# A linear-attention and feed-forward kernel on one core: raw weight loads opened by ScalarE, the first output cut in two, GpSimd's fills reordered, and another order of the first four steps

## The chip, the core and the metric

The kernel runs on one core of one Trainium2 chip. Five engines work side by side, each through its own queue of instructions in order: TensorE (PE, matrix products), VectorE (DVE, elementwise), ScalarE (ACT, activations and copies), GpSimd (POOL, fills, copies and some loads) and SyncE (SP, which issues most transfers). An instruction starts when it is first in its engine's queue and the semaphores that it waits for have been raised. Transfers between the chip's memory (HBM) and the core's (SBUF) run on 16 DMA engines, whichever engine issues them. Products land in PSUM.

The metric is the device time of one execution, in microseconds (us).

## The reference

The first half is a gated linear recurrence for 4 sequences with 8 heads, 768 positions and 48 channels; the second is a feed-forward layer on 3072 rows of 384, with a hidden width of 2048.

```python
f = 1.0 / (1.0 + np.exp(-f_logit))
state = np.zeros((B, H, D, D), dtype=np.float32)
for t in range(S):
    state = f[:, :, t, :, None] * state + np.einsum('bhd,bhe->bhde', k[:, :, t], v[:, :, t])
    y[:, :, t] = np.einsum('bhd,bhde->bhe', q[:, :, t], state)

x = y.transpose(0, 2, 1, 3).reshape(B * S, H * D)
h = x @ w_in
g = np.maximum(h, 0.0) + alpha * np.minimum(h, 0.0)
out = g @ w_out
```

Everything is float32. The rows of x that a position gives depend on all earlier positions of its sequence through `state` alone, so the positions are cut into chunks.

## The kernel before

**Steps.** The 768 positions are cut into 6 chunks of 128, the 4 sequences into 2 pairs. A step is one chunk of one pair; there are 12, numbered 0 to 11, the two pairs alternating. Steps 0 and 1 are the first chunks, which have no earlier state. Each step has these parts, generators that yield between pieces:

- P (`prepare`): loads of f, q, k and v (in steps 1 to 4 from GpSimd's queue, in the others from SP's), the sigmoid, and the products of gates over runs of 4 and 32 positions. It fills the tiles `kr`, `qd`, `us`, `ps`, `ss`, `k4`, and from them `q3`, `ks`, `kh`.
- S and T (`scores`, one for each sequence of the pair): products of keys and queries inside blocks of 32 positions (line 580), laid by masked copies on VectorE (L589 with the mask `mraw`, L615 with `mhalf` in first chunks, L599 with `mquad` in later ones) into `ad`.
- O (`carry`): products across blocks (L490, L512), the chunk's keys transposed (L529), the new state's part (L543), and `moved(0)`, which brings the state `vs` forward, in first chunks by ScalarE copies (L559).
- Y (`attend`): copies of `ad` into the attention matrix `A` (L623), the output of the attention (L634), its copy (L641), `moved(1)` on VectorE (L553, L557), and x transposed: in step 0 by products with a shifted identity `dense` (L653), in all others by small transfers (L664).
- K and M (`keys_moved`, `landed`): in later chunks the keys go through SBUF-to-SBUF transfers (L464).
- n (`network`): the feed-forward layer. Eight pieces of 12 matmul records (L679), each with ScalarE's `neg` (L684) and VectorE's `gate` (L686), and then products with `w_out`: in step 0 plain (L699), in the others by a scheme with 7 half-size products in place of 8 (L718).

**Weights.** w_in and w_out each come in 8 raw loads on SP's queue (L234) into 3 staging buffers. Of each, ScalarE makes a rounded float32 and a half-precision correction (L238, L239), and VectorE adds them as integers (L248). In the order the letters are a (raw load and ScalarE's two) and w (VectorE's) for w_in, b and g for w_out, W for sums of w_out's quarters (L784). A one-element ScalarE copy into the first staging buffer (L303, with q as its source) makes the first raw load wait until q has come.

**Order.** TensorE, VectorE, ScalarE and SP run a hand-made order: the string `START` is read word by word and each word advances one generator (`P0:4` advances P of step 0 four times). Steps from the fifth on follow a repeated pattern, `USUAL`. GpSimd is not in that list; its instructions stand in an order that a scheduler makes from the program's order. Fillers on TensorE, i (one product of 256 columns) and j (16 very small ones), write to a bank that nobody reads.

```python
        for key in ORDER:
            next(run[key] if key in run else pieces[key[0]])
```

**GpSimd before the first loads.** Its program is a row of fills and copies that build masks and zeros: `kr`, `fs`, `ones`, `mraw`, `mquad` (L171, L175), `mhalf` (L178, L183), `ad`, `A` (L190), the identity, `dense` (L197, L199); the fills of `us` for step 0 (L335, L336: zeros and ones in two parts of the tile) come from P, and so do the loads of the second step (L284, L293).

Of the kernel before, what the change touches and what calls it, by code (L numbers as in the profile page):

```python
# [8 lines left out]
F32 = mybir.dt.float32  # L9
I16 = mybir.dt.int16  # L10
# [7 lines left out]
C = 128  # L18
DB = 32
MASKED = (1, 0)  # L20

U = 2
CH = 64
NC2 = C // CH
NB = DB // 4
WP = 768
RAWS, LEADS = 3, 4
# [1 line left out]

BEGUN = 5  # L30
START = (
# [7 lines left out]
)  # L39
USUAL = "T:2 S:2 n:4 M T:2 S n P+ S n P+ n:3 Y O P+ O:2 Y O n P+ Y:2 P+ n:3 P+:3 K+"  # L40

LOOSE = ("a", "w", "b", "g", "W", "i", "j", "X")

def flat(start, usual, steps=12):
    out = []
# [15 lines left out]
def kernel(  # L61
# [30 lines left out]
    nc = tc.nc  # L92
    B, NC, _, HP, _ = qT.shape
    DM = v.shape[-1]
    H = 2 * HP
# [66 lines left out]

    mraw = const.tile([128, 4, NB, 4], F32, tag="mraw", name="mraw")
    nc.gpsimd.memset(mraw, 0.0)
    diag = lvl[:, 1].rearrange("p (i r) -> p i r", r=4)
    for d in range(4):
        nc.gpsimd.tensor_copy(mraw[:, d, :, d:4], diag[:, :, 0:4 - d])
    inq = const.tile([128, NB], F32, tag="inq", name="inq")
    nc.vector.tensor_reduce(inq, diag, mybir.AxisListType.X, ALU.add)
    mquad = const.tile([128, UW], F32, tag="mquad", name="mquad")  # L170
    nc.gpsimd.memset(mquad, 0.0)  # L171
    for m in range(1, NB):
        lo = UO[m] + (4 if m == 1 else 0)
        n = NB - m
        nc.gpsimd.tensor_copy(mquad[:, lo:lo + 4 * n].rearrange("p (i r) -> p i r", r=4),  # L175
                              inq[:, 0:n].unsqueeze(2).broadcast_to((128, n, 4)))
# [24 lines left out]
    first = {"raw": stage.tile([128, WP, 4], I16, tag="raw", name="w_in_raw0", bufs=RAWS)}  # L201

    def load_weights(dst, src, name):

        rows_ = NK if dst is w_in_sb else 1
        pieces_ = dst.shape[1] * dst.shape[2] // WP
        if rows_ == 1:
            dst = dst.rearrange("p a n -> p (a n)").unsqueeze(1)
        width = WP // rows_
        words = src.rearrange("p (a n) -> p a n", a=rows_).bitcast(I16)  # L220
        got = {}

        def of(n):
            return dst[:, :, n * width:(n + 1) * width]

        def by_row(t):
            return t.rearrange("p (a n) -> p a n", a=rows_)

        def upper(n):
            if not n and dst is w_in_sb:  # L230
                raw = first["raw"]
            else:
                raw = stage.tile([128, WP, 4], I16, tag="raw", name=f"{name}_raw{n}", bufs=RAWS)
            nc.sync.dma_start(out=raw.rearrange("p (a n) four -> p a (n four)", a=rows_)[:, :, 0:4 * width - 1],  # L234
                              in_=words[:, :, 4 * n * width + 1:4 * (n + 1) * width])

            lead = stage.tile([128, WP], F16, tag="lead", name=f"{name}_lead{n}", bufs=LEADS)
            nc.scalar.activation(lead, raw[:, :, 2].bitcast(BF16), AF.Copy, scale=0.5)  # L238
            nc.scalar.activation(as_int(n, I32), by_row(raw.bitcast(U32)[:, :, 0]), AF.Copy, scale=2.0 ** -13)  # L239
            got[n] = lead  # L240

        def as_int(n, dtype):
            t = of(n).bitcast(dtype)
            return t if dtype is I32 else t.rearrange("p a (n two) -> p a n two", two=2)[:, :, :, 1]

        def both(n):
            t = by_row(got.pop(n).bitcast(I16))
            nc.vector.tensor_tensor(as_int(n, I16), as_int(n, I16), t, ALU.add)  # L248
# [23 lines left out]
    def prepare(bp, c, x):  # L272
# [27 lines left out]
        qdv = [qd[:, :, QO[d]:QO[d] + NB * (4 - d)].rearrange("p g (i r) -> p g i r", r=4 - d) for d in range(4)]  # L300
        nc.scalar.copy(qd[:, :, 0:DB], q.rearrange("p (g t) -> p g t", t=DB))
        if not ahead:
            nc.scalar.copy(first["raw"].rearrange("p n four -> p (n four)")[:, 0:2].bitcast(F32), q[:, 0:1])  # L303
# [21 lines left out]


        ps = work.tile([128, NS], F32, tag="ps", name=f"ps_{i}", bufs=1)
        ut = work.tile([128, G * UW], F32, tag="us", name=f"us_{i}", bufs=1)
        if c:
            us = ut.rearrange("p (g t) -> p g t", g=G)  # L330
        else:

            at = (0, VW, VW + 16, VW + 16 + DB, VW + 16 + DB + NB)
            us, q16, k16, g16 = (ut[:, G * lo:G * hi].rearrange("p (g t) -> p g t", g=G) for lo, hi in zip(at, at[1:]))
            nc.gpsimd.memset(k16[:, :, 16:DB], 0.0)  # L335
            nc.gpsimd.memset(g16[:, :, 3:5], 1.0)  # L336
# [139 lines left out]
    def carry(bp, c, x):  # L476
# [21 lines left out]
        f64 = work.tile([128, U, H], F32, tag="f64", name=f"f64_{i}")  # L498
# [119 lines left out]
    def attend(bp, c, x):  # L618
# [5 lines left out]
            if j % 2:  # L624
                yield

        py = (more if (bp, c) == steps[0] else pairs)[0]
        for u in range(U):
            for hp in range(HP):
                for cc in range(NC2):  # L630
                    for par in range(2):
                        hd = 2 * hp + par
                        o = hp * C + CH * cc
                        nc.tensor.matmul(py[64 * par:64 * par + 64, u, o:o + CH],  # L634
                                         lhsT=vs[bp][:, cc, u, hd * D:hd * D + 64],
                                         rhs=A[:, u, par * HP + hp, CH * cc:CH * (cc + 1)],
                                         start=True, stop=True)
# [237 lines left out]
```

## Time and profile before

| | us |
|---|---|
| median of 3 runs | 602.92 (602.43 to 603.97) |
| the profiled execution | 602.81 |
| its span, first to last instruction | 601.0 |
| TensorE busy in the span | 575.6 (96%) |
| VectorE busy | 494.7 (82%) |
| ScalarE busy | 247.4 (41%) |
| GpSimd busy | 85.4 (14%) |

In the page's table of slices every digit is the busy share, in tenths, of one of 40 equal slices of the span, some 15 us each. The chain is the work that ended last, followed back from the last instruction. A row of the timeline gives the start in us from the beginning of the span, the duration, the engine, the line, the operation, the tile written and those read, the shapes, how many were merged, and in brackets the engine's idle time before the row and who ended it. A float32 matmul leaves two records, a transpose one. From about 120 us on the steps follow each other every 46.4 us (the products of L679 begin at 235.5, 281.9 and 328.4 us in steps 4, 5 and 6).

### The profile page before, as it was taken

The page shows a single profiled execution, that of the slowest core. Times are in us where ns is not written, and L with a number is a line of the kernel's source. Part 1 is how long each engine was busy: PE and PEld are TensorE (multiplying, and loading weights), DVE is VectorE, ACT ScalarE, POOL GpSimd, SP SyncE. Part 2 cuts the span into 40 slices and gives each one's busy share as a digit, 9 for nine tenths or more (in the row PEclk, how much of TensorE's full clock was granted, in tenths as well). Part 3 has the DMA queues.
Part 4 walks back from the last instruction along what each step waited for, and adds up shares of the span by engine and source line. Part 5 has one row for each costly group of instructions (what it writes and reads, how often), then busy time and mean ns, then how long its engine had stood idle before and what let it go on. Part 6 is the DMA issues. An engine that isn't in the chain of part 4 may idle for free.

```text
span 601.0 us, 18092 instructions
## 1 busy us (share of the span) xinstructions
PE 575.6 (96%) x7760; PEld 516.8 (86%) x7760; DVE 494.7 (82%) x998; ACT 247.4 (41%) x430; POOL 85.4 (14%) x162
## 2 busy tenths in 40 slices
PE   2489999999999999999999999999999999999997
PEld 1378667898899899899899899899899899899997
DVE  7989998997888779988988988988988987882351
ACT  5679952621461450550461451452343344232110
POOL 9210014013002103001200300300300300300000
PEclk9999999999999999999999999999999999999999
DMA  8778736015005302502601601601601511201000
GB/s 263 254 216 295 249 89 125 1 48 130 2 2 161 52 1 59 156 1 56 157 2 55 159 3 56 158 2 41 170 4 30 155 31 27 55 1 29 27 1 27
DMA packets 52880, 50.36 MB, mean 84 GB/s; under 512 B 26720, under 2 KB 43360, under 8 KB 52800
## 3 DMA queue, kind: packets, MB, share of 16 engines
q1 hardware_dynamic: 42784, 37.46, 21.7%
q0 software_dynamic: 5504, 9.90, 6.7%
q10 hardware_dynamic: 4512, 1.85, 1.3%
q8 instruction: 61, 1.00, 0.7%
q14 instruction: 19, 0.16, 0.1%
HBM read 36.21 MB, written 4.72 MB: 68 GB/s over the span
## 4 chain that ended last, share of the span: by engine, by line
PE 88%; DVE 7%; ACT 2%; POOL 1%; issue 1%; DMA 0%; DVEq 0%; ACTq 0%; POOLq 0%
PE ph L679 40%; PE pa L718 10%; PE pc L718 10%; PE pair L580 6%; PE pe L718 5%; PE pd L718 5%; PE pb L718 5%; PE pair L634 3%; PE pair L543 1%; DVE w_out_sb L248 1%; PE pair L512 1%; PE po L699 1%; DVE gate L686 1%; POOL mhalf L183 1%; DMA f<-in_fT 0%
## 5 line engine op out<-in xcount | busy, mean ns | idle before, releaser
L679 PE MATMUL ph<-xT,w_in_sb 128*128 128x256 f32 x1152 | 255.3, 381 | 1.4 <-DVE w_in_sb L248 1.4
L679 PEld LDWEIGHTS ph<-xT,w_in_sb 128*128 128x128 f32 x1152 | 216.9, 190 | 33.4 <-issue 2.4
L686 DVE SCALAR_TENSOR_TENSOR gate<-neg,om,ph 128x256 f32<-128x256 f32 x192 | 81.2, 476 | 33.0 <-ACT neg L684 33.0
L684 ACT ACTIVATE neg<-ph 128x512 f32<-128x512 f32 x96 | 56.1, 594 | 121.2 <-PE ph L679 101.6
L718 PE MATMUL pa<-w_out_sb,gate 128*128 128x192 f32 x352 | 62.1, 330 | 0.0
L718 PE MATMUL pc<-t,S 128*128 128x192 f32 x352 | 61.6, 328 | 0.0
L454 ACT COPY A<-q 48x512 f32<-48x512 f32 x44 | 27.1, 617 | 83.4 <-DVE q L408 82.9
L718 PEld LDWEIGHTS pa<-w_out_sb,gate 128*128 128x128 f32 x352 | 57.4, 190 | 1.3
L464 POOL DMA_DIRECT2D ksn<-kt x80 | 46.2, 586 | 85.9 <-DVE kt L422 61.3
L718 PEld LDWEIGHTS pc<-t,S 128*128 128x128 f32 x352 | 57.4, 190 | 0.4
L664 POOL DMA_DIRECT2D xT<-y x22 | 11.9, 544 | 287.5 <-ACT y L641 287.4
L599 DVE COPY_PREDICATED ad<-mquad,pair 128x224 f32<-128x224 int32 (+6 forms) x140 | 41.7, 299 | 4.1
L589 DVE COPY_PREDICATED ad<-mraw,pair 128x256 f32<-128x256 int32 (+1 forms) x96 | 41.2, 451 | 4.0 <-PE pair L580 0.8
L364 DVE TENSOR_TENSOR us<-us,fs 128x768 f32<-128x768 f32 (+5 forms) x60 | 36.9, 615 | 1.1
L765 DVE TENSOR_TENSOR S<-gate 128x512 f32<-128x512 f32 x44 | 30.3, 688 | 0.8
L718 PE MATMUL pe<-w_out_sb,S 128*128 128x192 f32 x176 | 30.6, 327 | 0.0
L718 PE MATMUL pb<-t,gate 128*128 128x192 f32 x176 | 30.4, 326 | 0.0
L718 PE MATMUL pd<-w_out_sb,S 128*128 128x192 f32 x176 | 30.4, 326 | 0.0
L623 ACT COPY A<-ad 32x512 f32<-32x512 f32 x48 | 29.4, 613 | 0.6
L641 ACT COPY y<-pair 128x512 f32<-128x512 f32 x22 | 11.8, 589 | 43.4 <-PE pair L634 43.4
L718 PEld LDWEIGHTS pe<-w_out_sb,S 128*128 128x128 f32 x176 | 28.8, 190 | 0.2
L718 PEld LDWEIGHTS pb<-t,gate 128*128 128x128 f32 x176 | 28.9, 190 | 0.0
(125 smaller groups left out, 710.6 us busy)
## 6 DMA issues: line engine op xcount, KB each, us to landing
w_out_raw<-in_w_out SPq DMA_DIRECT2D x8, 767.8 KB, 7.9
w_in_raw<-in_w_in SPq DMA_DIRECT2D x8, 767.2 KB, 9.5
out<-o SPq DMA_DIRECT2D x23, 192.0 KB, 1.9
q<-in_qT SPq DMA_DIRECT2D x8, 512.0 KB, 4.6
k<-in_kT SPq DMA_DIRECT2D x8, 512.0 KB, 7.1
f<-in_fT SPq DMA_DIRECT2D x7, 512.0 KB, 3.9
vs<-in_v SPq DMA_DIRECT2D x16, 192.0 KB
ksn<-kt SPq DMA_DIRECT2D x80, 32.0 KB, 2.2
```

Of the source, the lines that this page charges most:

```text
L364: nc.vector.tensor_tensor(us[:, :, UO[m]:UO[m] + 4 * n].rearrange("p g (i r) -> p g i r", r=4), us[:, :, skip:skip + 4 * n].rearrange("p g ...
L454: nc.scalar.copy(A[halves(cc)[1], :, par * HP:(par + 1) * HP, CH * cc:CH * (cc + 1)], q3[rows(par)].rearrange("p (u h c) s t -> p u h c (s ...
L464: (nc.gpsimd if a % 2 else nc.sync).dma_start(out=ksn[32 * b:32 * (b + 1)].rearrange("p u (h x) -> p (u h) x", h=HP)[:, :, 32 * a:32 * a + n],
L580: nc.tensor.matmul(to[DB * j:DB * (j + 1), par, hp * step + lo:hp * step + hi], lhsT=keys[r_, g * DB:(g + 1) * DB], rhs=by[r_, g, lo:hi], ...
L589: nc.vector.copy_predicated(adu[:, :, :, d:4], mraw[:, d, :, d:4].bitcast(I32).unsqueeze(1).broadcast_to((128, H, NB, n)), rv[:, :, QO[d]: ...
L599: nc.vector.copy_predicated(ad[:, u, :, :, 4 * m:DB], mquad[:, lo:lo + n].bitcast(I32).unsqueeze(1).unsqueeze(1).broadcast_to((128, 2, HP, ...
L623: nc.scalar.copy(A[s_].rearrange("p u h t -> p (u h) t")[:, :, s_], ad[s_].rearrange("p u r h t -> p (u r h) t"))
L679: nc.tensor.matmul(ph[:, j * T:(j + 1) * T], lhsT=w_in_sb[:, kt, m * 128:(m + 1) * 128], rhs=xT[:, kt], start=(kt == 0 and j == 0), stop=( ...
L684: nc.scalar.activation(neg, phv, AF.Relu, scale=-1.0)
L686: nc.vector.scalar_tensor_tensor(gate[:, m % NH, m // NH], neg[:, j], om[:, m:m + 1], phv[:, j], ALU.mult, ALU.add)
L718: nc.tensor.matmul(to[:, 0:DH], lhsT=of(f), rhs=by(f), start=(f == 0 and not more), stop=(f == NH - 1), skip_group_check=True)
L765: nc.vector.tensor_tensor(to, x_, y_, op)
```

## The change

It has four parts and an order.

- The first three raw tiles are made beforehand, and a function `opened` writes one element of a tile from ScalarE. The first is opened with q as before; a new letter e opens the second and third, with `inq` as the source, at two places of the order.
- The tile `us` of step 0 is made before the masks, and its two fills (`of_halves`) stand ahead of them; the fill of `A` goes to the end of the masks, and `mquad` is made in `quads_of_mask`, called in P of step 1 behind its loads.
- In step 0 the output of the attention (L634) is made in two halves of 16 matmuls, first the first half of the chunk for all heads, with a yield between.
- `START` is another order of steps 0 to 4. The filler j is gone from it, and both fillers i stand at its head.

```diff
-    "i P0:4 j T0 P0:2 S0 P0 a O0:2 T0 P1 P0 O0 T0 S0 O0 P1 S0 a O0 P1 T0 S0 P1 O0:2 Y0 i P1 Y0 O0 S1 w Y0 "
-    "a Y0 X a w O1 Y0 w O1 w S1 P1 a n0 w a:2 P1 n0 a T1 P1 P2 b S1 T1 S1 n0 w:2 n0 T1 O1 P2 T1 b P2 n0 w "
+    "P0 i P0 i P0 S0 P0:2 O0 e P0 O0 a P0 T0 e w P1 O0 T0 O0 a P1 O0:2 S0 T0:2 S0:2 P0 O0 P1 Y0 P1 Y0:2 "
+    "O0 Y0 a P1 Y0 P1 O1 a w X Y0 O1 w n0 a T1 S1:2 w:2 n0 a P2 w T1 P2 P1 a S1 n0 a S1 w n0:2 b T1 b O1 "
...
+    def of_halves(ut):
+
+        parts = [ut[:, G * lo:G * hi].rearrange("p (g t) -> p g t", g=G) for lo, hi in zip(at, at[1:])]
+        nc.gpsimd.memset(parts[2][:, :, 16:DB], 0.0)
+        nc.gpsimd.memset(parts[3][:, :, 3:5], 1.0)
+        return parts
+
+    first = {"us": work.tile([128, G * UW], F32, tag="us", name="us_first", bufs=1)}
+    first["parts"] = of_halves(first["us"])
...
-    nc.gpsimd.memset(mquad, 0.0)
-    for m in range(1, NB):
...
-    nc.gpsimd.memset(A, 0.0)
...
+    nc.gpsimd.memset(A, 0.0)
+
+    first["raw"] = [stage.tile([128, WP, 4], I16, tag="raw", name=f"w_in_raw{n}", bufs=RAWS) for n in range(RAWS)]
+
+    def opened(n, by):
+
+        nc.scalar.copy(first["raw"][n].rearrange("p n four -> p (n four)")[:, 0:2].bitcast(F32), by)
+
+    def quads_of_mask():
+
+        nc.gpsimd.memset(mquad, 0.0)
+        for m in range(1, NB):
+            lo = UO[m] + (4 if m == 1 else 0)
+            n = NB - m
+            nc.gpsimd.tensor_copy(mquad[:, lo:lo + 4 * n].rearrange("p (i r) -> p i r", r=4),
+                                  inq[:, 0:n].unsqueeze(2).broadcast_to((128, n, 4)))
...
+        if ahead == 1:
+            quads_of_mask()
...
+        chunks_first = (bp, c) == steps[0]
+        py = (more if chunks_first else pairs)[0]
+        each = [(u, hp, cc) for u in range(U) for hp in range(HP) for cc in range(NC2)]
+        for n, (u, hp, cc) in enumerate(sorted(each, key=lambda x: x[2]) if chunks_first else each):
+            if chunks_first and n == U * HP:
+                yield
...
+    pieces["e"] = (opened(n, inq[:, 0:1]) for n in range(1, RAWS))
```

More of the change, by code (lines that the diff above doesn't have):

```diff
@@ L31 @@
 START = (
[7 rows of a table removed]
[7 rows of a table added]
 )
 USUAL = "T:2 S:2 n:4 M T:2 S n P+ S n P+ n:3 Y O P+ O:2 Y O n P+ Y:2 P+ n:3 P+:3 K+"
-LOOSE = ("a", "w", "b", "g", "W", "i", "j", "X")
+LOOSE = ("a", "w", "b", "g", "W", "i", "j", "X", "e")
 def flat(start, usual, steps=12):
@@ L164 @@
     nc.gpsimd.memset(mraw, 0.0)
+    at = (0, VW, VW + 16, VW + 16 + DB, VW + 16 + DB + NB)
+    def of_halves(ut):
[5 more added lines that the diff above has]
+    first["parts"] = of_halves(first["us"])
     diag = lvl[:, 1].rearrange("p (i r) -> p i r", r=4)
@@ L170 @@
     mquad = const.tile([128, UW], F32, tag="mquad", name="mquad")
-    nc.gpsimd.memset(mquad, 0.0)
-    for m in range(1, NB):
[L173 to L176, printed above, removed]
     mhalf = const.tile([128, VW], F32, tag="mhalf", name="mhalf")
@@ L199 @@
         nc.gpsimd.tensor_copy(dense[:, (2 + par) * D:(3 + par) * D], ident[:, 64 * par:64 * par + D])
-    first = {"raw": stage.tile([128, WP, 4], I16, tag="raw", name="w_in_raw0", bufs=RAWS)}
+    nc.gpsimd.memset(A, 0.0)
[9 more added lines that the diff above has]
+                                  inq[:, 0:n].unsqueeze(2).broadcast_to((128, n, 4)))
     def load_weights(dst, src, name):
@@ L229, in upper @@
         def upper(n):
-            if not n and dst is w_in_sb:
-                raw = first["raw"]
+            if n < RAWS and dst is w_in_sb:
+                raw = first["raw"][n]
             else:
@@ L302, in prepare @@
         if not ahead:
-            nc.scalar.copy(first["raw"].rearrange("p n four -> p (n four)")[:, 0:2].bitcast(F32), q[:, 0:1])
+            opened(0, q[:, 0:1])
         yield
@@ L327, in prepare @@
         ps = work.tile([128, NS], F32, tag="ps", name=f"ps_{i}", bufs=1)
-        ut = work.tile([128, G * UW], F32, tag="us", name=f"us_{i}", bufs=1)
+        ut = work.tile([128, G * UW], F32, tag="us", name=f"us_{i}", bufs=1) if ahead else first["us"]
         if c:
@@ L331, in prepare @@
         else:
[L333 to L336, printed above, removed]
+            us, q16, k16, g16 = of_halves(ut) if ahead else first["parts"]
             x["q16"], x["k16"] = q16, k16
@@ L497, in carry @@
         q3, ks, kh, pre = (x[n] for n in ("q3", "ks", "kh", "pre"))
-        f64 = work.tile([128, U, H], F32, tag="f64", name=f"f64_{i}")
+        f64 = x["f64"] = work.tile([128, U, H], F32, tag="f64", name=f"f64_{i}")
         by64 = pre.rearrange("p (a c j) i -> p a c j i", c=NC2, j=2)
@@ L625, in attend @@
                 yield
[L627 to L637, printed above, removed]
+        chunks_first = (bp, c) == steps[0]
[4 more added lines that the diff above has]
+                yield
+            for par in range(2):
+                hd = 2 * hp + par
+                o = hp * C + CH * cc
+                nc.tensor.matmul(py[64 * par:64 * par + 64, u, o:o + CH],
+                                 lhsT=vs[bp][:, cc, u, hd * D:hd * D + 64],
+                                 rhs=A[:, u, par * HP + hp, CH * cc:CH * (cc + 1)],
+                                 start=True, stop=True)
         yield
```

10 rows, old and new, of the table START are left out of this document.

## The prediction, made before the changed kernel ran

> Line numbers are those of the kernel before. Durations come from its one profiled execution: 601.0 us of span and 1.8 around it make 602.81, 0.11 under the median of the runs (602.92). 0.3% of that, 1.8 us, is about what a measurement can tell from no change.
>
> **What bounds the kernel now.** I read the page first: the 40 slices and the chain that ended last.
>
> ```profile
> PE   2489999999999999999999999999999999999997
> PE 88%; DVE 7%; ACT 2%; POOL 1%; issue 1%; DMA 0%; DVEq 0%; ACTq 0%; POOLq 0%
> ```
>
> From the fourth slice of 15 us on TensorE is full and is nine tenths of the chain. What can be won lies in the first three slices: the time at which TensorE fills, and the work and waits that it has left then. So the second view is the timeline of VectorE and TensorE up to 90 us.
>
> ```profile
> 11.94 0.27 DVE L385 TENSOR_TENSOR us<-us,fs 128x64 f32<-128x64 f32 x1
> 13.70 0.69 DVE L387 TENSOR_TENSOR us<-k,us 128x512 f32<-128x512 f32 x1 [1.49 <-POOL us L336]
> ...
> 34.90 1.05 DVE L248 TENSOR_TENSOR w_in_sb<-w_in_sb,w_in_lead 128x768 int16<-128x768 int16 x1
> 37.64 0.95 DVE L553 TENSOR_TENSOR vs<-vs,f 48x768 f32<-48x768 f32 x1 [1.68 <-PE more L634]
> 38.62 1.12 DVE L557 TENSOR_TENSOR vs<-vs,more 48x384 f32<-48x384 f32 x2
> ```
>
> Between 4.4 us and the end of L557 at 39.75 VectorE has two real pauses: 1.49 for a fill by GpSimd and 1.68 for the first output (L634). TensorE's first large product follows L557 at once:
>
> ```profile
> 32.24 1.22 PE L790 MATMUL more<-ones 128*128 128x256 f32 x2
> 33.39 1.34 PE L580 MATMUL pair<-qd,k 48*32 48x80 f32 x64
> 34.66 2.97 PE L634 MATMUL more<-A,vs 128*64 128x64 f32 x64
> 37.56 1.58 PE L490 MATMUL pair<-us 48*32 48x16 f32 x128
> 39.89 2.83 PE L653 MATMUL xt<-y,dense 128*128 128x256 f32 x12 [0.75 <-DVE vs L557]
> ...
> 66.28 2.83 PE L679 MATMUL ph<-xT,w_in_sb 128*128 128x256 f32 x12 [1.36 <-DVE w_in_sb L248]
> ...
> 88.12 1.59 PE L580 MATMUL pair<-qd,k 48*32 48x80 f32 x128 [0.25 <-DVE vs L557]
> ```
>
> Three things are to be seen: L653 stands 0.14 behind VectorE's L557; a filler product (L790) and half of the second step's L580 stand ahead of the L634 for which VectorE waits; and from 39.89 on TensorE has two marked waits, 1.36 and 0.25, both for VectorE. GpSimd's queue explains the first pause: the fill of `us` stands behind thirteen masked copies.
>
> ```profile
> 5.58 3.05 POOL L175 COPY mquad<-inq 128x28 f32<-128x28 f32 x7
> 8.57 3.50 POOL L183 COPY mhalf<-inq 128x12 f32<-128x12 f32 x6
> 12.67 0.52 POOL L335 MEMSET us<- 128x512 f32 x1
> 13.46 0.21 POOL L336 MEMSET us<- 128x64 f32 x1
> 25.65 0.53 POOL L335 MEMSET us<- 128x512 f32 x1 [8.55 <-PE pair L580]
> ```
>
> **The change, part by part.**
>
> *GpSimd's fills first.* In the new order the two fills of `us` stand ahead of the masked copies and are done by about 2.7 us (0.52 + 0.21 behind fills that end at 2.0). L387 then waits for L385 alone, which ends at 12.21; dependent VectorE instructions follow 0.03 behind one another (5.15 + 0.40, then 5.58). Gain 1.45; the ends are 1.49 and, if the masked copies left at 4.9 to 8.4 hold something up, 1.0. The fill of `A` (1.81) goes behind them and ends near 10.7; its first reader (L519) comes at about 19. The seven copies of L175 (3.05) and their fill (0.20) go behind the loads of the second step, into the 8.55 that GpSimd idled before 25.65: nothing. Without that cover they would delay the second L335, whose reader L387 runs at 32.90, seven later.
>
> *First output in two halves, filler and half of L580 out of its way.* The new order has the same VectorE instructions between L387 and L557, only the masked copies L589 and L615 ahead of the second step's preparation. VectorE would come to L553 at 35.95 - 1.45 = 34.5. By then L634 must be through. Its second half needs ScalarE's copies of `vs` (L559), which end at 34.09 now. ScalarE ran without a pause from 20.52 to there, 13.6 us; in the new order the same work, with the first weights' 1.7 taken out into an earlier pause, starts at L519 near 19.3, so it ends between 32.3 and 32.9. Sixteen matmuls at 2.97/32 each are 1.5: 33.8 to 34.4, just in time. The pause of 1.68 goes; the ends are 1.68 and 0.6, should ScalarE be 1 us late. L653 then comes 1.45 + 1.68 earlier, at about 36.8.
>
> *What TensorE has left.* The 32 matmuls of L580 that ran ahead of L653 now run between the network's: 0.67 (their pace at 47.83). L490 stays ahead of L653; L790 and the short filler (0.42) at 3.26 sat in idle time: nothing but what is counted above.
>
> *The new order of steps 1 to 4.* Walking the new queues with these durations, VectorE meets every weight sum (L248) 2 us or more before the product that reads it, and the first of `w_out` about 0.9 before; the 1.36 does not come back, and about 0.4 does at L529. I take a gain of 1.0; the ends are 0, if new waits take the place of the old, and 1.6, both waits.
>
> *Raw loads opened by ScalarE.* Two copies like L303 (0.19 each) sit in ScalarE's pauses of 2.17 and 3.62: nothing. On SP the second and third raw load go from 7.63 and 8.29 to about 10.6 and 18.9, and the fourth, queued behind them, from 13.92 to 19.5. From issue to landing the trace has 7.35 for the second load and 11.15 for the fourth, which shared the engines with GpSimd's loads. So the second lands between 18.0 and 21.8, and ScalarE asks at about 20.3: 0 to 1.5 late, of which 0.5 reaches L553. I take 0, being nearer to the first row: fewer loads are under way. The third and fourth land by 30.7, asked at 32 and 35. GpSimd's f, q and v of the second step go out 2 us sooner, when L355 frees f at 11.5. k goes out 2 later, behind the second L580 (17.4): with the 10.33 of its row it lands at 27.7, against 28.3 where L354 wants it: nothing, and if it is late, one for one.
>
> *TensorE's speed.* The granted clock reads 1.00 in every slice, but matmuls are slow early on: eight transposes (L529) take 1.97 at 25.36 and 1.04 at 61.29, L634 2.97 at 34.66 and 2.09 at 80.42. L653 at 39.89 runs at the pace of L679 at 66.28, 2.83 for twelve. So the speed came up before L653, some 3.3 us after the stretch from 33.39 began in which TensorE hardly pauses. In the new order such a stretch begins at about 32.5 (second half of L634), or only at L653 if the small gaps before it count: L653 is at full speed at once (0), or slow for 3.3 us, losing half, 1.65. Neither row is nearer; I take 0.8 lost.
>
> [...]
>
> Sum: -1.45 - 1.68 + 0.67 - 1.0 + 0.8 = -2.66, and 602.81 - 2.66 = 600.15: I say 600.2.
>
> **The rivals.**
>
> *The pause comes back with another name.* ScalarE waits for the second raw load, L553 waits for `vs` again, and VectorE still holds up the products: -1.45 - 0.6 + 0.67 - 0 + 0.8 = -0.6, 602.2, no change. For it: ScalarE is in order and L634 has at most 0.7 to spare; against it: at the pace of its own row (7.35) that load lands 2.3 before ScalarE asks.
>
> *GpSimd's copies hold up VectorE.* The seven copies now run at about 18 to 21, beside VectorE's unbroken chain. If VectorE pays their 3.05 in full, -2.66 + 3.05 = +0.4, 603.2, no change. Against it: beside the same copies L310 took 0.96 at 6.89, and 0.96 at 24.83 without them; GpSimd's copies were the ones stretched. [...]
>
> *Slower: TensorE stays slow into the network.* The filler ahead of L580 is gone and the first output is cut in two with a pause of about 3 us between. If the speed comes up only after L653, the first group of L679 and the 64 matmuls of L580 (2.7 + 2.6 + 0.7 at full speed, twice that slow), 6.0 is lost: -3.46 + 6.0 = +2.5, 605.3. It decides the sign once more than 3.5 is lost, 7 us of slow running from 36.8. For it: the stretch of 22.35 to 27.3, with few gaps, did not raise the speed. Against: the wait of 1.36 at 64.9 did not lower it, and L653 is followed by products without a gap.
>
> *All of it.* Both waits of TensorE go and the speed is up at L653: -1.45 - 1.68 + 0.67 - 1.6 + 0 = -4.1, 598.7.
>
> **How the numbers follow.** Forecast 0.50, pause under another name 0.22, GpSimd's copies 0.05, slow TensorE 0.12, all of it 0.11. The forecast's bounds run from 599.2 to 601.5, a small part of it (0.03) within 0.3% of 602.92. Faster: 0.47 + 0.11 = 0.58; same: 0.03 + 0.22 + 0.05 = 0.30; slower: 0.12. The range reaches from 598.5, under the best case, to 603.8, over the two that change nothing, and leaves out the slow case.
>
> **What would show it.** In the profile after: no GpSimd wait at L387; L553 reached without a pause near 34.5; L653 at 36.8 and its twelve records in 2.8 (4 or more if slow); the first `po` (L699) near 65 where it was 68.95, with no TensorE wait over 0.5 from there to 90; from the fifth step on every product about 2.7 earlier. The prediction is wrong if L653 comes after 38, if ScalarE waits for a raw load before 32, or if TensorE's waits after L653 sum to more than the 1.6 of now.

## The result: 0.55% slower, and what the profile after shows

The median of four executions of the changed kernel is 606.25 us (605.46 to 607.27), beside 602.69 for the kernel before (four executions, 602.43 to 603.97): a ratio of 1.0055, 95% interval 1.0032 to 1.0078. The forecast was 600.2, faster. The profiled execution took 605.46, 2.65 more than the profiled execution before (602.81); its span is 603.7.

Line numbers from here on are those of the changed kernel: L404 was L387, L570 and L574 were L553 and L557, L597 was L580, L606 and L632 were L589 and L615, L507 was L490, L529 was L512, L358 was L341, L576 was L559, L653 was L634, L672 was L653, L698 was L679, L718 was L699.

First the page of the changed kernel: TensorE's 40 slices, the granted clock, the queue that carries code (packets, MB, share of the 16 DMA engines), and the chain that ended last.

```profile
PE   3479999999999999999999999999999999999997
...
PEclk9959999999999999999999999999999999999999
...
q8 instruction: 61, 1.00, 0.7%
...
PE 90%; DVE 4%; ACT 3%; issue 1%; ACTq 1%; DMA 1%; SPq 0%; DVEq 0%
```

As before, TensorE is full from the fourth slice on and is nine tenths of the chain: what happened lies in the first three slices. The third slice shows a granted clock of half, which no slice showed before. Next, VectorE's timeline, the rows that answer those shown of the kernel before, and the new waits.

```profile
12.31 0.69 DVE L404 TENSOR_TENSOR us_first<-k,us_first 128x512 f32<-128x512 f32 x1
...
21.74 3.81 DVE L606 COPY_PREDICATED ad<-mraw,pair 128x256 f32<-128x256 int32 x8 [1.53 <-PE pair L597]
26.74 2.05 DVE L632 COPY_PREDICATED ad<-mhalf,pair 128x224 f32<-128x224 int32 x6 [1.20 <-PE pair L597]
...
34.29 1.23 DVE L372 TENSOR_TENSOR us<-us,f 128x1024 f32<-128x1024 f32 x1 [0.77 <-ACT us L358]
...
38.44 0.95 DVE L570 TENSOR_TENSOR vs<-vs,f 48x768 f32<-48x768 f32 x1
```

Both pauses of the kernel before are gone: L404 starts at 12.31 without a wait (13.70 after 1.49 before), and L570 follows its predecessor at once (1.68 of wait before). But three new waits have come, 1.53 + 1.20 + 0.77 = 3.50, two of them for TensorE's score products. Without them VectorE would have been ready for L570 at 38.44 - 3.50 = 34.94; the prediction said 34.5. TensorE's timeline shows where the new waits come from:

```profile
13.76 1.38 PE L507 MATMUL more<-us_first 48*32 48x16 f32 x124 [3.18 <-DVE us_first L407]
...
15.00 0.74 PE L597 MATMUL pair<-qd,k 48*32 48x80 f32 x22
20.60 1.02 PE L597 MATMUL pair<-qd,k 48*32 48x80 f32 x38 [4.86 <-issue]
...
36.66 1.97 PE L653 MATMUL more<-A,vs 128*64 128x64 f32 x32 [2.47 <-ACT vs L576]
38.57 1.53 PE L507 MATMUL pair<-us 48*32 48x16 f32 x128
40.69 5.10 PE L672 MATMUL xt<-y,dense 128*128 128x256 f32 x12 [0.60 <-DVE vs L574]
```

Two things are new. In the midst of a batch of 64 equal matmul records, at 15.74, TensorE stops for 4.86 us, and the profile names nothing that it waits for ("issue"); 0.95 more of the same kind follows, up to 26.26. And L672 takes 5.10 where the same twelve records took 2.83 before. The chain of waits runs straight through the stop:

```profile
15.12 0.62 PE pair L597 x25
15.74 4.86 issue
20.60 1.02 PE pair L597 x38
```

Behind it the chain goes through ScalarE, which waits for the products (L529) that the stop has put off:

```profile
22.80 1.49 ACT L536 COPY A<-more 32x256 f32<-32x256 f32 x4 [5.44 <-PE more L529]
...
35.65 0.96 ACT L576 COPY vs<-more 48x384 f32<-48x384 f32 x2
```

L536 was L519 of the kernel before. The prediction had ScalarE begin it near 19.3 and end the copies of `vs` between 32.3 and 32.9; they ended at 36.6. The second half of the first output (L653), which waits for them, ran until 38.6. So ScalarE's delay alone would have held L570 back about as long as VectorE's three waits did: both ways lead from the same stop.

The account closes. L672 starts 0.80 later than before (40.69 against 39.89) and takes 2.27 longer. From 45 on TensorE hardly pauses: its marked waits sum to 0.54 where the kernel before had 1.36 + 0.25, so 1.07 is won, and the 32 products of L597 that ran ahead of the first output before now cost 0.67 (the prediction's figure, from their pace at 47.83). 0.80 + 2.27 - 1.07 + 0.67 = 2.67; the spans differ by 2.65, and the products of L698 in step 6 begin at 331.04 where they began at 328.36.

### The profile page after: what moved, and what is told of

It is laid out like the page before. It is cut to its first block, busy times and chain, and to the rows that moved or that the text cites. A ratio compares the mean times of both kernels' runs of the same rounds, so it can differ in the third digit from the quotient of the medians.

```text
span 603.7 us, 18029 instructions
## 1 busy us (share of the span) xinstructions
PE 577.2 (96%) x7728; PEld 517.9 (86%) x7728; DVE 494.8 (82%) x998; ACT 247.4 (41%) x432; POOL 81.6 (14%) x162
## 3 DMA queue, kind: packets, MB, share of 16 engines
q10 hardware_dynamic: 4512, 1.85, 1.4%
## 4 chain that ended last, share of the span: by engine, by line
PE 90%; DVE 4%; ACT 3%; issue 1%; ACTq 1%; DMA 1%; SPq 0%; DVEq 0%
PE ph L698 40%; PE pa L737 9%; PE pc L737 9%; PE pair L597 6%; PE pd L737 5%; PE pb L737 5%; PE pe L737 4%; PE pair L653 4%; PE po L718 4%; PE pair L560 1%; PE pair L529 1%; PE xt L672 1%; ACT us L358 1%; DVE ad L606 1%; ACTq L683 1%
## 5 line engine op out<-in xcount | busy, mean ns | idle before, releaser
L698 PE MATMUL ph<-xT,w_in_sb 128*128 128x256 f32 x1152 | 255.3, 381 | 0.2 <-DVE Csum L741 0.2
L698 PEld LDWEIGHTS ph<-xT,w_in_sb 128*128 128x128 f32 x1152 | 216.9, 190 | 32.2 <-issue 1.1
L606 DVE COPY_PREDICATED ad<-mraw,pair 128x256 f32<-128x256 int32 (+1 forms) x96 | 41.3, 452 | 5.4 <-PE pair L597 2.7
L597 PE MATMUL pair<-qd,k 48*32 48x80 f32 x1536 | 20.7, 244 | 9.9 <-DVE qd L330 5.1
L597 PEld LDWEIGHTS pair<-qd,k 48*32 48x32 f32 x1536 | 17.8, 109 | 13.8 <-issue 7.5
L741 DVE SCALAR_TENSOR_TENSOR Csum<-pc,Csum 128x192 f32<-128x192 f32 x22 | 7.8, 354 | 25.8 <-PE pc L737 25.6
```

The source lines that it names most:

```text
L597: nc.tensor.matmul(to[DB * j:DB * (j + 1), par, hp * step + lo:hp * step + hi], lhsT=keys[r_, g * DB:(g + 1) * DB], rhs=by[r_, g, lo:hi], ...
L606: nc.vector.copy_predicated(adu[:, :, :, d:4], mraw[:, d, :, d:4].bitcast(I32).unsqueeze(1).broadcast_to((128, H, NB, n)), rv[:, :, QO[d]: ...
L698: nc.tensor.matmul(ph[:, j * T:(j + 1) * T], lhsT=w_in_sb[:, kt, m * 128:(m + 1) * 128], rhs=xT[:, kt], start=(kt == 0 and j == 0), stop=( ...
```

## Two causes read from the traces

**Code.** The page has 61 packets of 16.4 KB on the queue q8 (1.00 MB) for 7728 matmul records and as many weight loads of TensorE: one packet for some 127 records. In the changed kernel the stop comes after 222 records: 4 of fillers and 64 of score products until 10.6, the 128 of L507, and 26 of the second batch (the rows left out between 13.76 and 15.00 are four more of L507 and four of L597). The kernel before stops at the same count: 2 + 32 of fillers, 128 of score products, and 60 of L490, behind which its timeline has

```profile
16.55 0.86 PE L490 MATMUL more<-us 48*32 48x16 f32 x68 [0.62 <-issue]
```

In both, TensorE goes on 1.5 to 1.6 us after a packet of q8 has landed (15.05 to 16.55 before, 19.01 to 20.60 after); the next such stop is at the 350th record in both (0.41 and 0.95), 128 further on, and runs below have one at the 478th, 128 further again. So the reading was, an estimate from these counts: TensorE stops behind its 222nd record until that packet is there, and the packet is asked for one packet's worth of records sooner, at the 94th. Before, the 94th record lay in the first batch of score products, at 10.3. In the new order the second batch stands behind L507, which waits for VectorE, and the short filler of 32 records is gone: the 94th record ran at 13.95. In both kernels the packet started 3.8 to 3.9 after that. (When a packet is asked for is in no record; it is inferred from the counts.)

**Clock.** The granted clock, in one stretch of the changed kernel and then of the kernel before (start to end, length, busy time of TensorE, its weight loads, VectorE, ScalarE and GpSimd, clock, DMA share, GB/s):

```profile
28.30:45.20 16.90, 11.45 (x267) 10.04 (x268) 15.82 (x27) 13.29 (x24) 2.67 (x4) 0.50 0.67 213
```

```profile
28.30:45.20 16.90, 13.54 (x347) 11.73 (x348) 14.12 (x27) 13.15 (x25) 1.93 (x3) 1.00 0.71 223
```

The clock's records have it at half from 28.23 to 45.29 after, and at full from 36.65 on before. (The 1.00 of the kernel before is for the recorded part alone: its records begin at 36.65, and until then its matmuls ran at the slow pace, eight transposes in 1.97.) All lengths between changes of the clock, in all the traces, are multiples of 3.41 us (3.41, 6.83, 10.24, 17.07, 559.8), and their phase differs from execution to execution (the change at 24.81 after and the one at 36.65 before lie 11.84 apart, 3.47 times 3.41). The reading was, an estimate from these lengths: each 3.41 us, a window, the clock is set by how busy TensorE was in the window that has just ended; what sets it is in no record. Before, TensorE ran from 32.24 (a filler, half of L580, the first output, L490) to 39.1 without a marked wait, 6.9 us, in which a whole window fits wherever it begins (2 x 3.41 = 6.8), and the 12 records of L653 took 2.83. After, the last such stretch ahead of L672 is 3.4 us long, from 36.66, and those records took 5.10 (an earlier one, from 20.60 to 25.3, stands ahead of a single window at full clock, 24.81 to 28.23).

## The experiments

Times are medians; the ratio is to the kernel before, run beside them on the same chip (602.7 to 603.0), with its 95% interval.

**One short filler back.** If the count decides, 32 records at the head, in idle time, move the stop.

```diff
-    "P0 i P0 i P0 S0 P0:2 O0 e P0 O0 a ...
+    "P0 i j P0 i P0 S0 P0:2 O0 e P0 O0 a ...
```

> The changed kernel with one short filler (16 very small products, 32 matmul records, 0.42 us) put back at the head of TensorE's order, in idle time. Theory CODE: TensorE's stop of 4.86 us at 15.7 stands at its 222nd record, in the kernel before as in the changed one, and ends 1.5 to 1.6 after a 16 KB packet of the instruction queue q8 has landed (15.05 and 19.01); that packet starts 3.8 after the 94th record, which ran at 10.3 before (in the first batch of score products) and at 13.95 after (in L507, which waits for VectorE). With 32 records ahead, the 94th is again in the first batch, near 10.2: its packet starts near 14, lands near 15, TensorE goes on at 16.6; the stop comes six records before the end of L507 and is 1.0 to 1.8 long. VectorE then has no wait at L606 and at most 0.5 at L632, L672 starts near 38.1, still at half speed (5.1), and the time is 602.9. Rival WAIT (the stop is a hidden wait for something else: a transfer, GpSimd's loads, VectorE): the stop stays from 15.7 to 20.6, the time 605.5.

604.48, ratio 1.0029 (1.0012 to 1.0046). TensorE's timeline of this run, and a row of VectorE's:

```profile
13.67 1.39 PE L507 MATMUL more<-us_first 48*32 48x16 f32 x122 [3.08 <-DVE us_first L407]
19.73 0.25 PE L507 MATMUL more<-us_first 48*32 48x16 f32 x3 [4.67 <-issue]
```

```profile
22.20 1.05 DVE L266 TENSOR_TENSOR w_in_sb<-w_in_sb,w_in_lead 128x768 int16<-128x768 int16 x1 [3.23 <-ACT w_in_sb L257]
```

The place was foretold to the record: the stop now stands after the 122nd of L507's 128 records. Its length was not: 4.67 in place of 1.0 to 1.8. The 94th record ran at 10.22, but the packet started at 17.09, 6.9 later. So CODE holds for the place, and the fixed 3.8 falls. As the last six records of L507 now came late, ScalarE's copies of them did too, and VectorE lost 3.23 at the weight sum in place of the waits at L606 and L632.

**Five short fillers.**

```diff
-    "P0 i P0 i P0 S0 P0:2 ...
+    "P0 i j:5 P0 i P0 S0 P0:2 ...
```

> The same with five short fillers (160 records, 2.1 us, in idle time until 9.3). CODE: the 94th record is a filler, near 4.5, and its packet has landed long before the 222nd, which is the 58th of the first batch of score products near 10.0; the 350th is the 58th of the second batch, behind L507, so a stop comes there, from about 15.6 to at most 16.6; none stands ahead of L507's end. Time 602.3 to 602.9. WAIT: the stop stays from 15.7 to 20.6, 605.5.

604.40, ratio 1.0032 (1.0008 to 1.0056). TensorE's timeline of the profiled execution, which at 607.07 was the longest of the seven:

```profile
11.44 0.48 PE L597 MATMUL pair<-qd,k 48*32 48x80 f32 x5 [0.83 <-issue]
...
22.08 0.24 PE L507 MATMUL more<-us_first 48*32 48x16 f32 x3 [6.97 <-issue]
```

Again the places fit (after 59 records of the first batch, where 58 were counted, and at the 350th record), and the lengths not. The first stop, 0.83, was not expected at all: its packet landed only at 10.03, though the 94th record had run at 4.09. The packet of the second stop started at 19.53, 9.3 after the 222nd record (10.27).

**The second and third raw load not opened.**

```diff
-    pieces["e"] = (opened(n, inq[:, 0:1]) for n in range(1, RAWS))
+    pieces["e"] = (None for n in range(1, RAWS))
```

> The changed kernel with ScalarE's two copies that open the second and third raw load left out: those loads go out behind the first one as in the kernel before. CODE: the 94th record stays at 13.95; the packet starts 3.8 later, as it does in both kernels although only one opens these loads; stop and time stay, 605.5 within 1. Rival TRAFFIC (loads that the openings put at 10 to 19 us delay the packet): the packet starts within 1.2 of the 94th record, the stop is under 2.5 long, time 603.

606.22, ratio 1.0065 (1.0041 to 1.0088): as the changed kernel. The 94th record at 13.78, the packet 4.3 later, the stop 5.14. The openings are no part of the loss; but GpSimd's loads were under way in this run as in the two before it.

**The first output whole.** This asks for the second cause: with both halves together TensorE runs without a pause for longer ahead of L672.

```diff
-        for n, (u, hp, cc) in enumerate(sorted(each, key=lambda x: x[2]) if chunks_first else each):
-            if chunks_first and n == U * HP:
+        for n, (u, hp, cc) in enumerate(each):
+            if chunks_first and n == 0:
                 yield
```

> The changed kernel with the first output whole: all 32 products where the second half stands. CLOCK (the granted clock rises to full some 4.4 to 4.6 after TensorE begins to run without a pause, and 0.6 or more of pause starts the count again): L653 runs from 36.6 without a pause for 3.9, L507 for 1.5, L672 starts at 42.1 and is at full speed by then or within 0.5, 2.8 to 3.3 long: its end at 44.9 to 45.4 is 0.4 to 0.9 sooner than now (45.8), time 604.6 to 605.1. Rival HALF (the half that runs early is worth its 1.98 on the path, and L672 is slow for another reason): L672 starts at 42.6 and takes 5.1, time 607.4.

606.58, ratio 1.0064 (1.0043 to 1.0084). TensorE's timeline of this run:

```profile
39.31 3.44 PE L653 MATMUL more<-A,vs 128*64 128x64 f32 x60 [3.92 <-ACT vs L576]
...
44.94 2.83 PE L672 MATMUL xt<-y,dense 128*128 128x256 f32 x12 [0.99 <-DVE vs L574]
```

L672 is at full speed, as CLOCK wanted; the time came out 1.5 over the 604.6 to 605.1 expected of that theory, and the median shows no gain. In the profiled execution the first load of q came late (ScalarE's first copy of it at 9.06, against 6.61 in the changed kernel's), and all that follows with it: less those 2.45, L672 ends at 45.3, where it ended at 45.8, so this execution shows 0.5 won. Why the median shows none of it stays open; for the speed of L672 the trace decides.

**The second step's loads held back.** The traces gave what the fixed 3.8 lacked: in each run so far loads kept the DMA engines busy from the 94th record until the packet started (a mean share of 0.87 or more; 0.98 before and 1.00 after, as the profile counts it). In the kernel before these were raw loads; in the changed kernel GpSimd's f, q and v, which go out at 11.8 to 14.7, were the most of it (0.97 of 1.19 MB). So these loads were made to wait.

```diff
-    "... O0 e P0 O0 a P0 T0 e w P1 O0 T0 ...
+    "... O0 e P0 O0 P1 a P0 T0 e w O0 T0 ...
...
+            if name != "k" and ahead == 1:
+                nc.scalar.copy(t[:, 0:1], inq[:, 0:1])
...
+            if ahead == 1:
+                nc.scalar.copy(vs[bp][t_, cc, 0, 0:1], inq[t_, 0:1])
```

> The changed kernel with the second step's f, q and v held back: four one-element ScalarE copies into their tiles, behind the copies that read L507, make GpSimd's loads wait until 15.9 (they go out at 11.8 to 14.7 now). Theory CODE AND TRAFFIC (TensorE stops at its 222nd record until a 16 KB packet of code lands; the packet is asked for at the 94th record and waits behind the loads that are under way on the DMA engines): the 94th record stays at 13.95, the packet starts within 1.5 of it, since only the end of the first raw load is under way, lands by 16.5, and TensorE goes on at 17 to 18 where it was 20.6. VectorE waits no more than 0.3 at L606 and 0.5 at L632 (1.53 and 1.20 now), L672 comes near 38.1, still slow (5.1); 602.9. Rival LATENCY (a packet takes 3.8 from request to start, loads or not): stop to 20.6, 605.5.

603.27, ratio 0.9999 (0.9975 to 1.0023): the loss is gone. GpSimd's load of f, TensorE's stop and L672 (whose line is now L676, and L597's L601):

```profile
17.31 0.90 POOL L304 DMA_DIRECT2D f<-in_fT  x1 [4.56 <-ACT vs L314]
```

```profile
18.50 1.02 PE L601 MATMUL pair<-qd,k 48*32 48x80 f32 x38 [1.57 <-issue]
...
38.62 4.61 PE L676 MATMUL xt<-y,dense 128*128 128x256 f32 x12 [0.56 <-DVE vs L578]
```

The packet started 1.15 after the 94th record, the stop shrank from 4.86 to 1.57, VectorE waits for TensorE only 0.16, and L672's products came at 38.62 although q was 1.3 late in this execution. They are still slow. TRAFFIC holds, LATENCY falls. The packets of code in all profiled executions, from the trace's record of DMA packets (us; "later" is from the 94th record to the packet's start; the stop is the idle time that the profile marks, and of the run with five fillers the row is that of the 222nd and 350th record):

```
                     record 94  packet starts  later  landed  TensorE goes on  stop
before                  10.30       14.16       3.9    15.05       16.55       0.62
after                   13.95       17.79       3.8    19.01       20.60       4.86
one short filler        10.22       17.09       6.9    18.13       19.73       4.67
five short fillers      10.27       19.53       9.3    20.69       22.08       6.97
not opened              13.78       18.11       4.3    19.26       20.71       5.14
whole                   16.11       20.71       4.6    22.00       23.31       5.41
three fillers           15.14       18.83       3.7    19.95       21.51       4.57
fills alone             12.26       17.11       4.9    18.19       19.61       3.09
order alone             15.33       19.05       3.7    20.05       21.71       4.58
loads held              15.13       16.28       1.2    17.21       18.50       1.57
held, three fillers     13.88       14.80       0.9    15.93       17.52       1.85
held, one filler        14.16       15.14       1.0    16.49       17.80       1.85
```

From landing to the next matmul it is always 1.3 to 1.7. In this table only the runs with the loads held have the packet start within 1.2. The traces also give the mean busy share of the 16 DMA engines between the record and the packet's start: 0.87 or more in the nine runs without the hold, and 0.56, 0.31 and 0.12 in the three with it.

The hold doesn't do away with the wait, it moves it. In the three held runs the loads go out later and meet the next packet of code: it starts 4.7 to 5.6 after the 350th record, at a DMA share of 1.04 to 1.05 (as the profile counts it, full), and TensorE stops for 2.32 (loads held), 3.19 (with three fillers) and 3.72 (with one) at the 478th record. In the changed kernel that packet started 1.9 later, at a share of 0.37, and there was no such stop.

**Three fillers between the halves**, in the changed kernel, loads as they were: the clock's cause alone. The new letter h is one filler.

```diff
+    def warm():
+        while True:
+            nc.tensor.matmul(more[0][:, 0].rearrange("p (h a t) -> p h a t", a=2, t=CH)[:, :, 1],
+                             lhsT=ones[:, 0:128], rhs=ones[:, 0:256], start=True, stop=True)
+            yield
...
-    "O0 Y0 a P1 Y0 P1 O1 ...
+    "O0 h:3 Y0 a P1 Y0 P1 O1 ...
```

> The changed kernel with three fillers (256 columns each, 2.56 at half speed) in TensorE's pause of 2.47 between the two halves of the first output. CLOCK (the granted clock is set anew every 3.41 us, to full if the window before was all but filled with matmuls, else to half): TensorE now runs without a pause over 0.4 from 32.2 to 40.1, more than two windows, so at least one is filled before L672: that takes 2.8 to 3.0 where it was 5.1; the code stop stays. L672 ends 2.2 to 2.8 sooner; 602.7 to 603.3. Rival SHAPE (the products of L672 are slow here for another reason, new places or transfers beside them): L672 stays at 5.1, 605.5 or 0.1 more.

604.78, ratio 1.0041 (1.002 to 1.0062). TensorE's timeline of this run:

```profile
36.15 2.84 PE L815 MATMUL more<-ones 128*128 128x256 f32 x6
...
41.83 2.83 PE L672 MATMUL xt<-y,dense 128*128 128x256 f32 x12 [0.57 <-DVE vs L574]
```

The second half takes 1.15 in place of 1.97, and L672 2.83 in place of 5.10: CLOCK holds, SHAPE falls. The time fell by less than expected (602.7 to 603.3). The fillers, 2.84 long, kept the second half back: ScalarE's copies of vs ended at 37.5 here, the fillers at 39.0; the second stop for code was 2.27, where it was 0.95; and a third came, 1.82, at the 478th record.

**Both**: the two edits above together, the loads held back and h:3.

> Both: the second step's loads held back and the three fillers. CODE AND TRAFFIC with CLOCK: -2.6 and -2.5 together, 600.0 to 600.8, near the time forecast for the change, with L672 at 37.5 to 38.5 and 2.8 to 3.0 long. If one of the two theories falls, 602.7 to 603.3; if both, 605.5.

602.46, ratio 0.9991 (0.9969 to 1.0013): better than either, but 1.7 short of what was expected. L672's products ran at full speed, at 38.83; the fillers ended at 36.4, while the copies of vs had ended at 33.5, so this time the fillers set the end; the stop at the 478th record put the first half ahead of them off.

**The fills alone**, in the kernel before: of_halves ahead of the masks, as in the change, and nothing else of it.

```diff
+    first = {"us": work.tile([128, G * UW], F32, tag="us", name="us_first", bufs=1)}
+    first["parts"] = of_halves(first["us"])
...
-            nc.gpsimd.memset(k16[:, :, 16:DB], 0.0)
-            nc.gpsimd.memset(g16[:, :, 3:5], 1.0)
+            us, q16, k16, g16 = of_halves(ut) if ahead else first["parts"]
```

> The kernel before with one part of the change alone: the two fills of the first step's us stand ahead of the masked copies. All agree that VectorE's wait of 1.49 at L387 goes. The prediction's term: 1.45 sooner to the end, 601.3. CODE AND TRAFFIC: L490 starts 1.4 sooner (13.7) but cannot end sooner than the code lands: it stops at its 60th record until some 1.5 after the packet, near 16.5 as before, so ScalarE's copies behind it and the products behind them come as before; VectorE loses its gain in a longer wait at L553 (1.68, up to 3.1); no change, 602.2 to 602.9. If GpSimd's loads, which go out sooner too, push the packet to 16 or later, slower: up to 605.

602.84, ratio 1.001 (0.9989 to 1.003): no change; a gain of 1.45 would be 0.9976. The profiled execution, at 605.16, lies 2.3 above that median. VectorE's timeline has no wait at that line (L395 here), and TensorE's has a stop in the products that read this part of `us` (L498 is L490 of the kernel before):

```profile
14.27 0.69 DVE L395 TENSOR_TENSOR us_first<-k,us_first 128x512 f32<-128x512 f32 x1
```

```profile
19.61 0.86 PE L498 MATMUL more<-us_first 48*32 48x16 f32 x68 [3.09 <-issue]
```

The reading is that what VectorE makes ready sooner, TensorE can't run before its code is there. The profile doesn't prove it for the median: q was 2.9 late in this execution, so late that the fill in its old place (done at 13.67) would not have held VectorE up either; and a second stop of 2.19 and transposing products at 4.54 in place of 2.83 lengthen it too.

**Held, with one filler in place of three.**

```diff
-    "O0 h:3 Y0 a P1 Y0 P1 O1 ...
+    "O0 h:1 Y0 a P1 Y0 P1 O1 ...
```

> The loads held back and one filler in place of three. In the run with three, the copies of vs ended at 33.51 and the first half of the first output at 33.52, so the fillers (33.52 to 36.4) pushed the second half back by 2.9; VectorE would have been ready for L672's line near 37.4, and it came at 38.83. CLOCK and the chain as read: with one filler (0.85 slow) the second half starts near 34.4, the next line at 37.4 to 38.0; it is at full speed (2.83) if a whole window of 3.41 fits in the stretch from 31.1, which it does in some 9 cases of 10, so 0.8 to 1.4 sooner than with three: 601.0 to 601.7. Rival: the second half still waits for ScalarE, the clock falls back, no gain: 602.5 to 603.5.

601.00 (12 executions, 600.26 to 603.96), ratio 0.9974 (0.9961 to 0.9987): faster than both kernels, by 0.26% and by about 0.8%. TensorE's timeline of this run, in which L653 is L657 and L672 is L676:

```profile
34.36 1.22 PE L819 MATMUL more<-ones 128*128 128x256 f32 x2
35.51 1.15 PE L657 MATMUL more<-A,vs 128*64 128x64 f32 x32
...
37.90 2.85 PE L676 MATMUL xt<-y,dense 128*128 128x256 f32 x12
```

The filler and the second half follow one another, and there is no marked pause from 31.96 to L672's products, which start at 37.90 and run at full speed; their end, 40.8, is 5.0 sooner than in the changed kernel. The stop for code of 3.72 is left ahead of it, at the 478th record. It hid in part behind ScalarE: without it the second half could have begun when the copies of vs ended, at 33.8, in place of 35.51.

**The order alone**, in the kernel before: the new START, without the two openings, the first output whole.

```diff
-    "i P0:4 j T0 P0:2 S0 P0 a O0:2 T0 P1 P0 ...
+    "P0 i P0 i P0 S0 P0:2 O0 P0 O0 a P0 T0 w P1 O0 T0 O0 a P1 O0:2 S0 T0:2 S0:2 P0 O0 P1 Y0 P1 Y0 "
+    "O0 Y0 a ...
```

> The kernel before with the new order alone: first output whole at the place of the second half, GpSimd's program and the raw loads as before. The prediction's terms: no filler and no half of L580 ahead of L634, the two later waits gone, 601.5 or less. CODE AND TRAFFIC: the 94th record lies in L490 behind VectorE (15.2 with GpSimd's late fill), when the loads of GpSimd are just going out: the packet starts 3 to 5 later (18.5 to 20.5), TensorE's stop in the second batch ends at 21 to 23, VectorE waits for it; L653 comes near 42 to 43 and is at full speed, since the whole first output and L490 run ahead of it without a pause for over 5: 605 to 607.

606.82, ratio 1.0069 (1.0045 to 1.0093): the whole loss, without any other part of the change. TensorE's timeline of this run:

```profile
21.71 1.02 PE L580 MATMUL pair<-qd,k 48*32 48x80 f32 x38 [4.58 <-issue]
...
43.34 2.83 PE L653 MATMUL xt<-y,dense 128*128 128x256 f32 x12 [0.96 <-DVE vs L557]
```

The stop is there, although GpSimd's fills and its loads of f, q and v stand as before: the 94th record runs at 15.33, when raw loads are still under way and GpSimd's begin, and the packet starts 3.7 later. VectorE waits 1.18 and 0.40, and 1.62 more for the whole output at L553; the transposing products start at 43.34, at full speed, since here the whole output runs just ahead of them.

## Why the prediction was wrong, point by point

- *GpSimd's fills first, -1.45.* The wait went as said (12.31 against 13.70). The term failed in counting it on to the end: the products that read this part of `us` (L507) ended at 15.2, where they ended at 17.4 before, but TensorE stopped for code in the batch right behind them. The fills alone changed nothing (602.84).
- *First output in two halves, -1.68.* L570 was reached without a pause, as said, but at 38.44 and not at 34.5. The step that failed is that the products were taken to run as soon as VectorE and ScalarE had made their inputs, with no wait of TensorE's own; that they stood first in the queue, with nothing shown that they waited for, was not enough here, by 4.86. So "the new order has the same VectorE instructions between L387 and L557" is true, but 3.50 of new waits stand among them, behind TensorE's stop of 4.86 and the smaller one of 0.95 (the 0.77 by way of ScalarE). And ScalarE's work that "starts at L519 near 19.3" started at 22.80, after 5.44 of waiting for L529's products; its copies of `vs` ended at 36.6, not between 32.3 and 32.9. The trace of the kernel before did show a stop of that kind, 0.62 with nothing named, and the prediction passed over it.
- *L672 near 36.8.* It came at 40.69, 3.89 late. With the loads held and one filler it came at 37.90.
- *Half of L580 behind, +0.67, and TensorE's later waits, -1.0.* Right, as far as the account shows: it closes with 0.67, and the waits fell by 1.07.
- *TensorE's speed, +0.8, bounds 0 to 1.65.* Mis-sized: 2.27. The upper bound took the clock to rise 3.3 us after a stretch begins; it rose 4.6 after L672 began here (at 45.29), and 3.0 to 4.8 after it in the other runs in which these products began slow: its changes lie multiples of 3.41 apart, and at no fixed time behind the stretch.
- *Raw loads and GpSimd's loads, nothing.* The openings cost nothing, as said. That f, q and v went out 2 us sooner was counted as harmless; in the changed kernel they are what the packet of code waited behind (held back: 1.2 in place of 3.8). They are not the only loads that do it: with the order alone the packet was as late (3.7).
- *The rivals.* "The pause comes back with another name" was right that the output would wait for ScalarE (2.47 at the second half) and wrong in why: ScalarE waited for TensorE's products and for no raw load. "TensorE stays slow into the network" named the right side, and L672 was slow (5.10), but slowness ended with it (the next 12 records, L698, took 2.75); 2.27 alone would not have decided the sign, for which 3.5 was needed. What decided it was in none of the rivals. "GpSimd's copies hold up VectorE": the seven copies took 1.01 (3.05 before), and VectorE paid next to nothing (its eight predicated copies of L606 beside them took 3.81, where they took 1.85 + 1.87 before).

With the terms as measured: -2.66 + 3.89 (L672's start) + 1.47 (its speed beyond 0.8) - 0.07 = +2.63, against 2.65.

## What to carry to other kernels

An idle time of TensorE with no releaser in the midst of equal products is worth a count of the records ahead of it: here it stood at the same count in both kernels, and still did with 32 or 160 records put ahead, and TensorE went on 1.3 to 1.7 after a packet of code had landed. The new order, which put the 94th record behind a wait (13.95 in place of 10.30), cost 4.86 in the middle of the second batch with GpSimd's loads on the DMA engines at that time, and 1.57 with them held. Before a gain on another engine is carried on to the end, look in the trace whether the products that would use it have their code. And where a string of short fillers or small products is taken away, look how long TensorE ran without a marked pause ahead of the next long product: here 6.9 us ahead of twelve records that took 2.83, and 3.4 ahead of the same twelve at 5.10.

## What the runs showed of the hardware that was not expected

- TensorE's packet of code (16.4 KB, 0.9 to 1.4 us on the way in the table) came late while loads kept the DMA engines busy: it started 0.9 to 1.2 after the 94th record with GpSimd's loads held (a mean share of 0.12 to 0.56 until then), 3.7 to 6.9 without (0.87 or more), and 9.3 after the 222nd record with five short fillers. Why a packet starts just when it does among the packets of the loads was not tried.
- Where GpSimd and VectorE ran side by side, GpSimd's copies took longer in one case than in the other, and VectorE's product shown did not: the seven copies of L218 took 1.01 at 22.93 in the changed kernel, beside VectorE's predicated copies out of PSUM, and 3.41 at 8.86, beside its products of two SBUF tiles, in the run with the loads held and one filler. One of these products (L371, there L375) took 1.23 in both.
- Executions of one and the same kernel differ by up to 5.8 us (601.3 to 607.1 with five short fillers). In the profiled ones ScalarE's first copy of q starts anywhere between 5.69 and 9.06, as its load lands, and all that follows moves with it; the clock's windows fall differently too. How much of the spread each makes was not measured.
- The granted clock stayed at full through windows with 0.75 (the kernel before), 0.96 (the order alone) and 0.99 of pause (the first output whole), and fell after one with 1.04 (the fills alone, window from 38.0 to 41.4); it did not rise on a window with 0.60 of pause (the changed kernel, 38.5 to 41.9), and rose on one with 0.45 (one short filler, 40.1 to 43.5).
